# Sink keys of a banded attention: from shared float32r products to float32 products on 16 lanes inside the value step, with new order parameters

## The chip, the cores and the metric

The kernel runs on one core of a Trainium2 chip. The metric is device microseconds (us) of one execution; lower is better. PE is TensorE (PEld its weight loads), DVE is VectorE, ACT is ScalarE, POOL is GpSimd and SP is SyncE, which here issues the DMAs. L12 is line 12 of the kernel before.

## The reference

Two attentions follow each other. The first has 4 batches, 8 heads, 768 positions and head size 64; a query sees the last 128 positions and, besides, the first 4 positions (the sinks):

```python
is_sink = pos[None, :] < int(n_sink)                # n_sink = 4
in_window = (rel >= 0) & (rel < int(window))        # window = 128
scores = np.where(is_sink | in_window, scale * (q @ k.T), -1e9)
attn_out = softmax(scores) @ v                      # per batch and head
```

Its output, heads side by side (512 columns), is the input x of the second: 4 experts, each a causal attention over all 768 positions with its own wq, wk, wv (512x64) and wo (64x512). A gate picks 2 of the 4 experts per position and weights them.

```python
ye = softmax(causal(scale * (x @ wq[e]) @ (x @ wk[e]).T)) @ (x @ wv[e]) @ wo[e]
out += mask[..., None] * w[:, :, kk:kk + 1] * ye
```

## The kernel before

**Units.** The work is cut into 24 units. 16 are of the first kind (`first`, `band_rows`): a batch and a pair of heads. 8 are of the second kind (`second`, `wide_rows`): a batch and a pair of experts; ahead of a batch's first one `values` computes x times wv and the gate, and after its second one `store` multiplies by wo and writes out. Every unit walks over 6 rows of 128 queries.

**A banded row.** TensorE computes the scores of each of two heads (L449): 128 queries against 260 columns, which are 128 positions of the block before, 4 sink keys, and 128 positions of the row's own block. VectorE adds the mask and takes the minimum of the negated scores (L646), ScalarE takes the exponential with its row sum (L651), VectorE inverts the sum (L489, L490), and GpSimd scales the row p by it. For rows 2 to 5 GpSimd first adds the two 128 columns of p to each other (`merge`, L664), since the value products use the block before for both and correct the own block by a difference of values `dv` (L626). Rows 2 and 3, and rows 4 and 5, go on as a pair: `transposed_band` transposes both rows' p on TensorE (L530), copies the result out of PSUM as it is (`evacuate`, L351 on ScalarE or L353 on VectorE) and masked (L533 on VectorE), and multiplies both by values (`acc.add`, L482). A value product has 64 weight columns, and the two heads write the two halves of the partitions of `acc`. It is a float32 product, which stands as two records in the trace.

**The sinks.** The 4 sink columns of rows 2 to 5 are not part of that pair. GpSimd keeps them, scaled, in `psk` (`keep`, L658), which has three copies for a split of float32 into two float32r parts: 3 copies x 4 rows x 2 heads x 4 sinks = 96 columns. Twice per unit (once for row 2, once for rows 3 to 5) TensorE transposes `psk` (L684), ScalarE copies it to `sk` as float32r (L686), VectorE subtracts the rounded part on 32 lanes (L688), and a step of its own, `sinks`, adds one product per row to `acc` (L482, `acc<-sk,vs`): 96 lanes, 128 weight columns, both heads at once, one record each. Its weights `vs` are made by GpSimd once per unit from the first 4 values of every head (`spread`, L617, 96x512), and `psk` is cleared once per unit (L619). `sink_values` makes the copies of those values on 96 lanes once, at the start: two DMAs (L312), two float32 products (L320), copies and differences (L323, L325). When a half unit is complete, `finish` splits `acc` into two float32r parts of x (L334, L339).

**What sets the order.** Each engine runs its instructions in the order in which the program issues them, and `Plan.emit` writes that order out when the program is built: a list scheduler of made-up engine times that always takes the step that could start first, and among those the one of lowest priority number. A step's number is the place of its row in the sequence of units less a lead (`LEAD_S` for scores, `LEAD_E` for exponentials, `LEAD_N` for scaling; `WIDE_S`, `WIDE_E`, `WIDE_N` likewise), or plus `AV_LAG` for the value products; `PREP_*`, `VALUES`, `STORE`, `WP` and `WS` place the preparations, stores and weights. `STAY` is added to the number of a step on TensorE that would change the way in which the array is cut (`mode`), so a larger one lets equal steps gather. `ORD` and `LAST` are the sequences of units of a batch.

Of the kernel before, what the change touches and what calls it, by code (L numbers as in the profile page):

```python
# [29 lines left out]
STAY = 7.6  # L30
# [115 lines left out]
def kernel(  # L146
# [35 lines left out]
             "v2": 1, "y0": 1, "y1": 1, "p": 6, "dv": 2, "pt": 6, "psk": 2, "sk": 2, "vs": 2, "o": 2,  # L182
# [3 lines left out]
        {"space": bass.MemoryType.PSUM} if tag in ("s", "t", "acc") else {}))) for tag, n in rings.items() if tag not in ("kz", "st")}  # L186
# [27 lines left out]
    if banded:  # L214
# [15 lines left out]
        gsel = consts.tile([96, 8], F32, name="gsel")  # L230
        nc.gpsimd.memset(gsel, 1.0)
        for c in range(3):
            g = gsel[c * 32:c * 32 + 32]
            nc.gpsimd.affine_select(out=g, in_=g, pattern=[[-4, 8]], compare_op=OP.is_ge, fill=0.0,
                                    base=0, channel_multiplier=1)
            nc.gpsimd.affine_select(out=g, in_=g, pattern=[[4, 8]], compare_op=OP.is_ge, fill=0.0,
                                    base=3, channel_multiplier=-1)
# [64 lines left out]
    def sink_values():  # L302
        vr = buf("v2", [8, B * HP, D])
        vp = consts.tile([96, B * HP * D], F32R, name="vp")
        copies = consts.tile([8, 12, 8], F32, name="copies")
        nc.gpsimd.memset(copies, 1.0)
        nc.gpsimd.affine_select(out=copies, in_=copies, pattern=[[0, 12], [1, 8]], compare_op=OP.is_equal,
                                fill=0.0, base=0, channel_multiplier=-1)

        def load():  # L310
            for e in range(2):
                nc.sync.dma_start(vr.t[e * 4:e * 4 + 4], bass.AP(tensor=v.tensor, offset=v[0, e].offset,  # L312
                                                               ap=[[D, 4], [2 * S * D, B * HP], [1, D]]))
        ld = plan.step(SINK_VALUES, {SP: 950}, load, new=[vr], fifo="v2", moves=200)
        done = []
        for n in range(0, B * HP * D, 512):
            ns = slice(n, min(n + 512, B * HP * D))
            t = buf("t", [128, 4, 128])
# [201 lines left out]
    def transposed_band(prio, accs, i, ps, normed, value, diff):  # L520

        t = new_t()
        whole, part = buf("pt", [128, 2, 2, 128]), buf("pt", [128, 2, 2, 128])

        def tr():
# [18 lines left out]
        for acc in {id(x): x for x in accs}.values():  # L546
            acc.steps.append(s)
# [373 lines left out]
```

## Time and profile before

| | us |
|---|---|
| median of 3 runs | 473.53 (472.79 to 474.91) |
| the profiled execution: own time | 478.79 |
| its span, first to last instruction | 477.1 |
| PE busy | 451.3 (95%) |
| PEld / DVE / ACT / POOL busy | 388.2 / 344.0 / 320.0 / 276.3 |
| mean granted TensorE clock | 0.982 |

The profiled execution took 1.7 us more than its span, and 5.3 us more than the median. Its span is what all views divide up. Busy times of PE are modelled ends of pipelined products, so the distance from one start to the next tells more of the price of a product than its duration.

### The profile page before, as it was taken

To read this page: it belongs to the slowest core of one execution; us is meant where nothing else is said; L and a number is where in the kernel's file an instruction comes from. 1 tells how busy PE (TensorE), PEld (TensorE's weight loads), DVE (VectorE), ACT (ScalarE), POOL (GpSimd) and SP (SyncE) were. 2 spreads that over 40 slices of the span, in tenths; PEclk is the share of its full clock that TensorE was granted. 3 is DMA by queue.
4 is the path that set the end of the run, shared out by engine and by line. 5 is a ranking of instruction groups with operands and counts; after the bars stand their busy time and mean duration, and the time that the engine had idled before them with its cause. 6 is when DMAs were issued, how large, how long until landed. Compare 5 with 4: busy or idle time off the path is not lost.

```text
span 477.1 us, 11401 instructions
## 1 busy us (share of the span) xinstructions
PE 451.3 (95%) x3732; PEld 388.2 (81%) x3732; DVE 344.0 (72%) x1334; ACT 320.0 (67%) x917; POOL 276.3 (58%) x485
## 2 busy tenths in 40 slices
PE   6998989999899999999989999899999999999996
PEld 4676668898688978998878978799888788998775
DVE  6587786577779787467778878775977975367773
ACT  4778986547759778546758789775577865246640
POOL 8668998345836666526565746762647472015660
PEclk9978999999999999999989999999999999999999
DMA  8858596411635678222424986543112412214012
GB/s 175 160 123 165 134 246 145 101 34 34 145 91 134 170 186 219 61 69 66 101 68 103 211 210 164 119 103 93 40 43 59 103 47 89 63 38 101 0 42 93
DMA packets 95715, 51.89 MB, mean 109 GB/s; under 512 B 84648, under 2 KB 84648, under 8 KB 95656
## 3 DMA queue, kind: packets, MB, share of 16 engines
q1 hardware_dynamic: 95656, 51.16, 45.3%
q8 instruction: 30, 0.49, 0.4%
q14 instruction: 29, 0.24, 0.2%
HBM read 21.01 MB, written 6.29 MB: 57 GB/s over the span
## 4 chain that ended last, share of the span: by engine, by line
PE 69%; DVE 15%; ACT 8%; issue 3%; POOL 2%; DMA 1%; SPq 0%; POOLq 0%; DVEq 0%; ACTq 0%
PE acc L482 16%; PE s L449 14%; PE t L764 12%; PE t L507 10%; PE t L835 6%; PE t L790 6%; DVE p L646 3%; PE t L738 3%; DVE pt L533 2%; PE t L530 2%; ACT pt L351 2%; DVE p L583 2%; ACT p L593 1%; ACT qs L412 1%; ACT p L651 1%
## 5 line engine op out<-in xcount | busy, mean ns | idle before, releaser
L449 PE MATMUL s<-ks,qs 64*128 64x260 f32 (+6 forms) x416 | 109.8, 352 | 3.1 <-DVE st L646 2.2
L651 ACT ACTIVATE p<-p,st 128x260 f32<-128x260 f32 (+1 forms) x192 | 93.9, 497 | 18.5 <-DVE st L646 16.6
L600 POOL TENSOR_TENSOR p<-p,st 128x128 f32<-128x128 f32 (+5 forms) x96 | 87.6, 933 | 3.6 <-POOL st L493 0.2
L593 ACT ACTIVATE p<-p,st 128x128 f32<-128x128 f32 (+5 forms) x96 | 64.0, 668 | 33.0 <-DVE st L583 27.2
L646 DVE CUSTOM_DVE_ANT_0 p<-s,bmask 128x260 f32<-128x260 f32 (+1 forms) x192 | 73.6, 399 | 14.3 <-PE s L449 10.1
L351 ACT ACTIVATE pt<-t 128x512 f32<-128x512 f32 (+1 forms) x104 | 54.9, 536 | 42.3 <-PE t L507 28.4
L449 PEld LDWEIGHTS s<-ks,qs 128*128 128x128 f32 (+1 forms) x416 | 65.0, 203 | 19.9 <-DVE st L583 5.5
L449 PE MATMUL s<-kz,qs 128*128 128x260 f32 (+4 forms) x272 | 79.4, 305 | 0.1
L671 POOL TENSOR_TENSOR p<-p,st 128x256 f32<-128x256 f32 x96 | 65.7, 688 | 17.6 <-DVE st L490 10.0
L507 PE MATMUL t<-ident,p 128*128 128x128 f32 x432 | 65.6, 286 | 3.5 <-DVE ql L416 2.8
L664 POOL TENSOR_TENSOR p<-p 128x256 f32<-128x256 f32 x64 | 46.8, 734 | 34.7 <-ACT p L651 34.5
L493 POOL TENSOR_TENSOR st<-st,gate 128x2 f32<-128x2 f32 x48 | 9.4, 195 | 85.6 <-DVE st L490 77.1
L507 PEld LDWEIGHTS t<-ident,p 128*128 128x128 f32 x432 | 50.9, 146 | 9.9 <-POOL p L600 4.2
L583 DVE CUSTOM_DVE_ANT_0 p<-s,cmask 128x512 f32<-128x512 f32 (+3 forms) x96 | 51.6, 552 | 4.3 <-PE s L449 4.1
L449 PEld LDWEIGHTS s<-kz,qs 128*128 128x128 f32 x272 | 51.9, 191 | 1.7 <-DMA kz<-kl 0.2
L412 ACT ACTIVATE ks<-t 128x768 fp32r<-128x768 f32 (+2 forms) x76 | 38.7, 552 | 17.1 <-PE t L764 13.6
L412 ACT ACTIVATE qs<-t 128x768 fp32r<-128x768 f32 (+1 forms) x48 | 36.4, 758 | 18.6 <-PE t L764 14.9
L482 PE MATMUL acc<-pt,vn 128*64 128x128 f32 x448 | 41.2, 291 | 4.2 <-ACT pt L351 3.4
L482 PE MATMUL acc<-pt,v 128*64 128x128 f32 x672 | 44.5, 280 | 0.3 <-DVE pt L353 0.2
L353 DVE COPY pt<-t 128x512 f32<-128x512 f32 (+1 forms) x56 | 35.4, 632 | 12.8 <-PE t L507 12.5
L482 PEld LDWEIGHTS acc<-pt,v 128*64 128x64 f32 x672 | 36.3, 137 | 7.6 <-issue 3.4
L790 PE MATMUL t<-wvh,x 128*128 128x260 f32 x192 | 38.5, 287 | 0.4 <-DVE st L489 0.4
(106 smaller groups left out, 959.7 us busy)
## 6 DMA issues: line engine op xcount, KB each, us to landing
qs<-ql SPq DMA_DIRECT2D x40, 192.0 KB, 3.8
vn<-in_v_dram SPq DMA_DIRECT2D x32, 192.0 KB, 3.6
out_dram<-o SPq DMA_DIRECT2D x24, 256.0 KB, 2.3
qn<-in_q_dram SPq DMA_DIRECT2D x30, 192.0 KB, 3.3
kn<-in_k_dram SPq DMA_DIRECT2D x30, 192.0 KB, 4.0
ks<-ks SPq DMA_DIRECT2D x24, 197.0 KB, 4.3
kz<-kl SPq DMA_DIRECT2D x24, 197.0 KB, 4.6
ks<-ks SPq DMA_DIRECT2D x16, 192.0 KB, 3.2
```

The costliest lines, as they stand in the source:

```text
L351: nc.scalar.activation(dst(), src(), AF.Copy)
L412: nc.scalar.activation(dst(), src(), AF.Copy, scale=mul)
L449: nc.tensor.matmul(o, lhs, rhs, start=n == 0, stop=n == (2 if self.flat else 1))
L482: nc.tensor.matmul(o if e is None else o[e * 64:e * 64 + 64], lhs, rhs, start=first and e is not None, stop=last and i % 3 == 2)
L507: nc.tensor.transpose(t.t[:, 2 * e + c, :], block(e, c), ident)
L583: nc.vector.tensor_tensor_reduce(out=p.t[:, cs], in0=s.t[:, :(c1 - c0) * 128], in1=mask[:, cs], scale=1.0, scalar=st.t[:, 3, es] if c0 els ...
L593: nc.scalar.activation(x, x, AF.Exp, bias=st.t[:, 0, es], scale=-1.0, accum_out=st.t[:, 1, es])
L600: nc.gpsimd.tensor_mul(x, x, st.t[:, 2, e:e + 1].to_broadcast([128, n * 128]))
L646: nc.vector.tensor_tensor_reduce(out=p.t[:, e, a:], in0=s.t[:, a:RW], in1=row_mask[i][:, a:], scale=1.0, scalar=BIG, op0=OP.add, op1=OP.mi ...
L651: nc.scalar.activation(x, x, AF.Exp, bias=st.t[:, 0, e:e + 1], scale=-1.0, accum_out=st.t[:, 1, e:e + 1])
L671: nc.gpsimd.tensor_mul(x, x, st.t[:, 2, :][:, :, None].to_broadcast([128, 2, z - a]))
L790: nc.tensor.matmul(ps()[:, :VW], X[b, c].t[:, a, qs], W["wv"][w][:, c, :], start=c == 0 and n == 0, stop=c == NCH - 1 and n == 2)
```

## The change

The sinks stay in float32. `psk` becomes a ring of 4 constant tiles of 128x128 that are cleared once at the start; a tile holds, in its first 16 columns, two rows x two heads x 4 sinks, and the other columns stay zero. It is transposed once per pair of rows and copied by `evacuate` on either engine, with no second part. `vs` becomes a ring of 2 constant 128x(4x64) tiles whose first 16 lanes GpSimd fills per unit (16x256 elements). The step `sinks` is gone: `av` of `transposed_band` adds, for each row and head, a float32 product with 64 weight columns, 128 lanes and 128 moving columns, and so waits for the copy `moved_sk` and for `vs` as well. `sink_values` loads 16 lanes with four DMAs and computes nothing. All order parameters change, and one sequence of units: the last batch runs `p0 p1` ahead of its own units 2 and 3 rather than between them. The diff, cut:

```diff
-STAY = 7.6
+STAY = 9.08
...
     rings = {"qn": 2, "kn": 2, "vn": 3, "ql": 1, "kl": 1, "qs": 2, "ks": 2, "kz": 2, "x": 6,
-             "v2": 1, "y0": 1, "y1": 1, "p": 6, "dv": 2, "pt": 6, "psk": 2, "sk": 2, "vs": 2, "o": 2,
+             "v2": 1, "y0": 1, "y1": 1, "p": 6, "dv": 2, "pt": 6, "psk": 4, "sk": 2, "vs": 2, "o": 2,
              "gate": 2, "gates": 1, "st": 6, "s": 3, "t": 3, "acc": 2}
...
-        gsel = consts.tile([96, 8], F32, name="gsel")
...
+        gsel = consts.tile([16, 4], F32, name="gsel")
...
+        sink_ring = {}
+        for tag, shape in (("psk", [128, 128]), ("vs", [128, 4, D])):
+            tiles = [consts.tile(shape, F32, name=f"{tag}{n}") for n in range(rings[tag])]
+            for t in tiles:
+                nc.gpsimd.memset(t, 0.0)
+            sink_ring[tag] = itertools.cycle(tiles)
...
-        vr = buf("v2", [8, B * HP, D])
-        vp = consts.tile([96, B * HP * D], F32R, name="vp")
-        copies = consts.tile([8, 12, 8], F32, name="copies")
...
+        vp = consts.tile([16, B * HP, D], F32, name="vp")
...
-            for e in range(2):
...
-            mm = plan.step(SINK_VALUES, {PE: 870}, lambda ps=ps, ns=ns: nc.tensor.matmul(
...
-            h = plan.step(SINK_VALUES, {ACT: 500}, lambda ps=ps, ns=ns: nc.scalar.activation(vp[:, ns], ps(), AF.Copy),
...
-            done.append(plan.step(SINK_VALUES, {DVE: 600}, lambda ps=ps, ns=ns: nc.vector.tensor_sub(
...
+            for r in range(2):
+                for e in range(2):
+                    nc.sync.dma_start(vp[r * 8 + e * 4:r * 8 + e * 4 + 4],
+                                      bass.AP(tensor=v.tensor, offset=v[0, e].offset, ap=[[D, 4], [2 * S * D, B * HP], [1, D]]))
+        return vp, [plan.step(SINK_VALUES, {SP: 1900}, load, moves=400)]
...
+    def transposed_band(prio, accs, i, ps, normed, value, diff, sinks):
...
+        psk, kept, vs, made_vs = sinks
+        ts, sk = new_t(), buf("sk", [128, 128])
...
+        tt = plan.step(prio, {PE: 109}, lambda: nc.tensor.transpose(ts.t[:, 0, :], psk.t, ident), kept, [ts, sk], [psk])
+        moved_sk = evacuate(prio, lambda: sk.t, lambda: ts.t[:, 0, :], 128, [tt], [ts, sk])
...
-                for c in range(2):
+                for c in range(3):
                     for e in range(2):
-                        acc.add(i + r, e, diff[0](i + r, e) if c else value[0](i + r - 1, e), (part if c else whole).t[:, r, e, :])
+                        if c == 2:
+                            acc.add(i + r, e, vs.t[:, 2 * r + e, :], sk.t, True)
+                        else:
+                            acc.add(i + r, e, diff[0](i + r, e) if c else value[0](i + r - 1, e), (part if c else whole).t[:, r, e, :])
...
+        s = plan.step(prio + AV_LAG, {PE: 1308}, av, [moved, tri, moved_sk, made_vs] + value[1] + diff[1], new,
+                      [whole, part, sk, vs] + value[2] + diff[2] + [acc.b for acc in both if acc.b not in new],
                       fifo="av", mode="cols")
...
-        psk = buf("psk", [128, 3, 4, 2, 4])
-        vs = buf("vs", [96, 8, D], F32R)
+        vs = Buf("vs", lambda: next(sink_ring["vs"]))
...
-            vp = SINKS[0].bitcast(F32)[:, number, :]
-            nc.gpsimd.tensor_mul(vs.t, vp[:, None, :].to_broadcast([96, 8, D]), gsel[:, :, None].to_broadcast([96, 8, D]))
-        made_vs = plan.step(prio0, {POOL: pool_cost(512)}, spread, SINKS[1], [vs], fifo="vs")
-        cleared = plan.step(prio0, {POOL: 150}, lambda: nc.gpsimd.memset(psk.t, 0.0), (), [psk], fifo="psk")
-        kept = []
...
+            nc.gpsimd.tensor_mul(vs.t[:16], vp[:, None, :].to_broadcast([16, 4, D]), gsel[:, :, None].to_broadcast([16, 4, D]))
+        made_vs = plan.step(prio0, {POOL: pool_cost(256)}, spread, SINKS[1], [vs], fifo="vs")
...
-                def keep(i=i, p=p, st=st):
-                    nc.gpsimd.tensor_mul(psk.t[:, :, i - 2], p.t[:, None, :, 128:SW].to_broadcast([128, 3, 2, 4]),
-                                         st.t[:, 2, :][:, None, :, None].to_broadcast([128, 3, 2, 4]))
-                kept.append(plan.step(prio - LEAD_N, {POOL: 190}, keep, [r, cleared], (), [p, st, psk]))
...
+                if i % 2 == 0:
+                    psk = Buf("psk", lambda: next(sink_ring["psk"]))
+
+                def keep(i=i, p=p, st=st, psk=psk):
+                    nc.gpsimd.tensor_mul(psk.t[:, i % 2 * 8:i % 2 * 8 + 8].rearrange("p (e s) -> p e s", e=2), p.t[:, :, 128:SW],
+                                         st.t[:, 2, :][:, :, None].to_broadcast([128, 2, 4]))
+                kept = [plan.step(prio - LEAD_N, {POOL: 190}, keep, [r], [] if i % 2 else [psk], [p, st] + ([psk] if i % 2 else []),
+                                  fifo=None if i % 2 else "psk")]
...
-            for g in ([0] if i == (3 if joined < NB else 2) else [1] if i == NB - 1 else []):
-                ts, sk = new_t(), buf("sk", [96, 128], F32R)
-                tt = plan.step(prio, {PE: 109}, lambda ts=ts: nc.tensor.transpose(
-                    ts.t[:96, 0, :], psk.t.rearrange("p c i e s -> p (c i e s)"), ident), kept[:1] if not g else kept[:], [ts, sk], [psk])
-                h = plan.step(prio, {ACT: 158}, lambda sk=sk, ts=ts: nc.scalar.activation(sk.t, ts.t[:96, 0, :], AF.Copy),
-                              [tt], (), [sk, ts])
-                lw = plan.step(prio, {DVE: 320}, lambda sk=sk, ts=ts: nc.vector.tensor_sub(
-                    sk.t[64:96], ts.t[64:96, 0, :], sk.t[64:96].bitcast(F32)), [h], (), [sk, ts])
...
-                def sinks(span=span, sk=sk, acc=accs[g]):
-                    for ii in span:
-                        lhs = vs.t[:, 2 * (ii - 2):2 * (ii - 2) + 2, :].rearrange("p e d -> p (e d)")
-                        acc.add(ii, None, lhs, sk.t, True)
-                accs[g].steps.append(plan.step(prio, {PE: 50 + 112 * len(span)}, sinks, [lw, made_vs, accs[g].steps[-1]], (),
-                                           [sk, vs, accs[g].b], fifo="av"))
...
-    LEAD_S, LEAD_E, LEAD_N = 6, 1.6, 2.7
-    WIDE_S, WIDE_E, WIDE_N = 7.9, 2.1, 3.3
-    UNIT_1, UNIT_2, AV_LAG, JOIN = 10, 24, 3.8, 0
-    SINK_VALUES = 6
+    LEAD_S, LEAD_E, LEAD_N = 9.36, 3.77, 3.75
+    WIDE_S, WIDE_E, WIDE_N = 8.23, 2.76, 1.78
+    UNIT_1, UNIT_2, AV_LAG = 10.36, 24.87, 3.27
+    SINK_VALUES = 3.68
...
-    LAST = "0 1 2 p0 p1 3 c0 c1"
+    LAST = "0 1 p0 p1 2 3 c0 c1"
...
-    PREP_0, PREP_1, PREP_2, VALUES, STORE = 9.6, 23.9, 24.6, 11.2, 3.8
-    WP, WS = 3.4, 5.8
+    PREP_0, PREP_1, PREP_2, VALUES, STORE = 7.63, 26.46, 22.81, 10.54, 5.79
+    WP, WS = 2.88, 7.16
```

The program's orders show where this moves work. First the start of unit 0's pair of rows 2 and 3 on PE; `psk` is transposed, `v`,`copies` is the product of `sink_values`, `acc<-sk,vs` the sinks. Before:

```order
L320 MATMUL t<-v_262,copies 96x512
L449 MATMUL s<-ks,qs 128x260 x6
L320 MATMUL t<-v_262,copies 96x512
L684 MATMUL t<-ident,psk 96x128
L449 MATMUL s<-ks,qs 128x260 x6
L530 MATMUL t<-ident,p 128x128 x4
L482 MATMUL acc<-pt,vn 64x128 x2
L482 MATMUL acc<-pt,dv 64x128 x2
L482 MATMUL acc<-pt,vn 64x128 x2
L482 MATMUL acc<-pt,dv 64x128 x2
L449 MATMUL s<-ks,qs 128x260 x6
L482 MATMUL acc<-sk,vs 128x128
```

In the changed program, the same place:

```order
L525 MATMUL t<-ident,psk_174 128x128
L519 MATMUL t<-ident,p 128x128 x4
L437 MATMUL s<-ks,qs 128x260 x6
L470 MATMUL acc<-pt,vn 64x128 x2
L470 MATMUL acc<-pt,dv 64x128 x2
L470 MATMUL acc<-sk,vs_182 64x128 x2
L470 MATMUL acc<-pt,vn 64x128 x2
L470 MATMUL acc<-pt,dv 64x128 x2
L470 MATMUL acc<-sk,vs_182 64x128 x2
L437 MATMUL s<-ks,qs 128x260 x6
L525 MATMUL t<-ident,psk_175 128x128
```

The two products of `sink_values` are gone, and the sink products stand inside the run of value products instead of behind the next row's scores.

Next, on PE, rows of unit p1 of batch 2 (`v_4722` before, `v_4891` changed: its values) among preparations (`qn`, `kn`) and rows of other units. Before:

```order
L482 MATMUL acc<-pt,v_4722 64x128 x14
L738 MATMUL t<-ident,kn 128x128 x3
L507 MATMUL t<-ident,p 128x128 x4
L449 MATMUL s<-ks,qs 128x512
L449 MATMUL s<-kz_204,qs 128x512
L449 MATMUL s<-ks,qs 128x128
L449 MATMUL s<-kz_204,qs 128x128
L449 MATMUL s<-ks,qs 128x512
L449 MATMUL s<-kz_204,qs 128x512
L482 MATMUL acc<-pt,v_4722 64x128 x4
```

In the changed program, the same place:

```order
L720 MATMUL t<-ident,kn 128x128 x3
L495 MATMUL t<-ident,p 128x128 x18
L437 MATMUL s<-ks,qs 128x260
L437 MATMUL s<-kz_206,qs 128x260
L470 MATMUL acc<-pt,v_4891 64x128 x18
L437 MATMUL s<-ks,qs 128x260
L437 MATMUL s<-kz_206,qs 128x260
L437 MATMUL s<-ks,qs 128x260
L437 MATMUL s<-kz_206,qs 128x260
```

Transposes and value products of several steps now stand together: runs of 18 where runs of 4 and 14 stood. Over all of PE's order there were 76 runs of value products, sinks apart, and there are now 63.

Last, POOL's first instructions (`gsel` is the selector for `vs`, `cmask` the causal mask, `copies` the weights of the products of `sink_values`). Before:

```order
L234 AFFINE_SELECT gsel<-gsel 32x8
L236 AFFINE_SELECT gsel<-gsel 32x8
L252 MEMSET cmask 128x768
L253 AFFINE_SELECT cmask<-cmask 128x128
L261 MEMSET tril 128x16
L262 AFFINE_SELECT tril<-tril 128x16
L306 MEMSET copies 8x96
L307 AFFINE_SELECT copies<-copies 8x96
L619 MEMSET psk 128x96 x2
```

In the changed program, the same place:

```order
L233 AFFINE_SELECT gsel<-gsel 16x4
L235 AFFINE_SELECT gsel<-gsel 16x4
L241 MEMSET psk_174 128x128
L241 MEMSET psk_175 128x128
L241 MEMSET psk_176 128x128
L241 MEMSET psk_177 128x128
L241 MEMSET vs_182 128x256
L241 MEMSET vs_183 128x256
L257 MEMSET cmask 128x768
L258 AFFINE_SELECT cmask<-cmask 128x128
L266 MEMSET tril 128x16
L267 AFFINE_SELECT tril<-tril 128x16
L618 TENSOR_TENSOR dv<-vn 128x4x64 x2
```

The clearing of `psk` and `vs` has moved to the start, and the second and third group of `gsel` and `copies` are gone.

## Rows read from the trace of the kernel before

**Rows 1.** The page, busy time, share of the span and instructions of each engine

```profile
PE 451.3 (95%) x3732; PEld 388.2 (81%) x3732; DVE 344.0 (72%) x1334; ACT 320.0 (67%) x917; POOL 276.3 (58%) x485
```

**Rows 2.** Windows: stretch, us, busy by engine (PE PEld DVE ACT POOL), PEclk, DMA

```profile
0.00:40.00 40.00, 34.56 (x222) 24.61 (x222) 27.47 (x116) 27.71 (x90) 30.21 (x75) 0.91 0.77 153
40.00:80.00 40.00, 34.58 (x314) 27.52 (x315) 32.34 (x135) 34.73 (x114) 35.70 (x65) 0.96 0.85 189
...
440.00:477.00 37.00, 32.74 (x277) 25.47 (x275) 22.88 (x71) 15.65 (x39) 16.90 (x23) 1.00 0.12 44
```

**Rows 3.** Windows, shorter stretches, the same columns

```profile
20.00:30.00 10.00, 10.00 (x62) 6.12 (x59) 6.94 (x26) 6.54 (x22) 6.68 (x11) 0.70 0.60 131
...
50.00:60.00 10.00, 8.81 (x80) 6.28 (x76) 9.09 (x39) 9.70 (x33) 10.00 (x17) 1.00 0.66 153
60.00:70.00 10.00, 8.11 (x84) 6.60 (x85) 8.21 (x35) 8.55 (x28) 9.91 (x20) 1.00 1.10 247
```

**Rows 4.** Timeline of PE: start us, us, what, records; a pair's value products, three sinks

```profile
61.03 0.39 PE L482 MATMUL acc<-pt,vn 128*64 128x128 f32 x4
61.25 0.39 PE L482 MATMUL acc<-pt,dv 128*64 128x128 f32 x4
61.56 0.56 PE L482 MATMUL acc<-sk,vs 96*128 96x128 f32 x3
61.95 0.62 PE L507 MATMUL t<-ident,p 128*128 128x128 f32 x4
```

**Rows 5.** Timeline of PE, from scores into value products, and one sink product

```profile
68.36 0.28 PE L449 MATMUL s<-ks,qs 128*128 128x260 f32 x1
68.48 0.28 PE L449 MATMUL s<-kz,qs 128*128 128x260 f32 x1
68.69 0.44 PE L482 MATMUL acc<-pt,vn 128*64 128x128 f32 x4
...
69.71 0.33 PE L482 MATMUL acc<-sk,vs 96*128 96x128 f32 x1
69.88 0.34 PE L449 MATMUL s<-ks,qs 128*128 128x260 f32 x1
```

**Rows 6.** Timeline of PE at the start, the products of `sink_values`

```profile
21.60 1.09 PE L320 MATMUL t<-v,copies 8*96 8x512 f32 x2
22.62 0.64 PE L449 MATMUL s<-ks,qs 64*128 64x260 f32 x6
23.19 1.35 PE L320 MATMUL t<-v,copies 8*96 8x512 f32 x2
24.47 0.45 PE L684 MATMUL t<-ident,psk 128*96 128x128 f32 x1
```

**Rows 7.** Timeline of PE, from value products into transposes

```profile
376.01 0.66 PE L482 MATMUL acc<-pt,v 128*64 128x128 f32 x8
376.60 0.71 PE L507 MATMUL t<-ident,p 128*128 128x128 f32 x4
```

**Rows 8.** Groups by form: what, count | busy us, mean ns | idle before

```profile
L671 POOL TENSOR_TENSOR p<-p,st 128x256 f32<-128x256 f32 x80 | 49.0, 615 | 11.2 <-DVE st L490 7.4 <-ACT p L651 2.2 <-ACT vp L323 1.3
...
L617 POOL TENSOR_TENSOR vs<-vp,gsel 96x512 fp32r<-96x512 f32 x16 | 16.6, 1041 | 0.0
...
L658 POOL TENSOR_TENSOR psk<-p,st 128x24 f32<-128x24 f32 x64 | 14.4, 228 | 5.0 <-DVE st L490 3.7 <-ACT x L334 0.9
...
L688 DVE TENSOR_TENSOR sk<-t,sk 32x128 fp32r<-32x128 f32 x32 | 9.3, 289 | 1.0
...
L686 ACT ACTIVATE sk<-t 96x128 fp32r<-96x128 f32 x32 | 8.5, 267 | 1.3 <-PE t L684 1.3
...
L619 POOL MEMSET psk<- 128x96 f32 x16 | 2.8, 176 | 11.8 <-PE t L684 11.8
```

**Rows 9.** Waits: who waited for whom, us in total, times, longest

```profile
PEld acc L482 <- ACT pt L351: 5.9, 10, 1.2
```

**Rows 10.** Timeline of SP, DMA issues of the sink values

```profile
9.13 0.80 SPq L312 DMA_DIRECT2D v<-in_v_dram  x2
```

More of the change, by code (lines that the diff above doesn't have):

```diff
@@ L185 @@
     pools = {tag: ctx.enter_context(tc.tile_pool(name=tag + "_", bufs=n, **(
-        {"space": bass.MemoryType.PSUM} if tag in ("s", "t", "acc") else {}))) for tag, n in rings.items() if tag not in ("kz", "st")}
+        {"space": bass.MemoryType.PSUM} if tag in ("s", "t", "acc") else {}))) for tag, n in rings.items() if tag not in ("kz", "st", "psk", "vs")}
     consts = ctx.enter_context(tc.tile_pool(name="consts", bufs=1))
@@ L229 @@
                                 base=0, channel_multiplier=-1)
-        gsel = consts.tile([96, 8], F32, name="gsel")
+        gsel = consts.tile([16, 4], F32, name="gsel")
         nc.gpsimd.memset(gsel, 1.0)
[L232 to L237, printed above, removed]
+        nc.gpsimd.affine_select(out=gsel, in_=gsel, pattern=[[-4, 4]], compare_op=OP.is_ge, fill=0.0,
+                                base=0, channel_multiplier=1)
+        nc.gpsimd.affine_select(out=gsel, in_=gsel, pattern=[[4, 4]], compare_op=OP.is_ge, fill=0.0,
+                                base=3, channel_multiplier=-1)
+        sink_ring = {}
[4 more added lines that the diff above has]
+            sink_ring[tag] = itertools.cycle(tiles)
     else:
@@ L626, in differences @@
                 nc.gpsimd.tensor_sub(dv.t[:, :, e, :], value[2][0].t[:, 2:, e, :], value[2][0].t[:, 1:NB - 1, e, :])
-        differ = joined < NB and plan.step(prio0 - LEAD_E, {POOL: 1390}, differences, value[1], [dv], value[2], fifo="dv")
+        differ = plan.step(prio0 - LEAD_E, {POOL: 1390}, differences, value[1], [dv], value[2], fifo="dv")
         accs, rows = [Acc(), Acc()], {}
@@ L700 @@
+            else:
+                rows[i] = (p, nm, kept)
+                if i % 2:
+                    before = rows[i - 1]
+                    transposed_band(prio, [accs[(i - 1) // 3], acc], i - 1, [before[0], p], [before[1], nm], value,
+                                    (lambda i, e: dv.t[:, i - 2, e, :], [differ], [dv]), (psk, before[2] + kept, vs, made_vs))
+                    finish(prio, accs[i // 4], i // 4)
     X, X_READY, Y, Y_READY, V2, V2_READY, WT, WT_READY = ({} for _ in range(8))
@@ L745, in first @@
         if banded:
-            band_rows(prio0, step, pair, value, b * HP + hp, finish, 2 if b >= JOIN else NB)
+            band_rows(prio0, step, pair, value, b * HP + hp, finish)
         else:
```

44 lines of the change are left out of this document (10 added, 34 removed).

## The prediction

> **What bounds the kernel now.** I read the busy shares first, then the windows, then the timeline of TensorE for prices, then the groups of the engines that feed it. TensorE is busy 451.3 of 477.1 us [rows 1], far ahead of VectorE, ScalarE and GpSimd. So the time is TensorE's work plus 25.8 us in which it stands. The windows tell where it stands [rows 2]: 5.4 us in the first 40 (which holds the start), 5.4 us between 40 and 80, 4.3 us in the last 37, and by difference 10.7 us spread over the 360 us between. From 50 to 70 us GpSimd is busy 10.00 and 9.91 of 10 us, ScalarE up to 9.70 [rows 3]: there the banded rows of batches 0 and 1 run with no expert work to fill TensorE, and GpSimd is the pace. Elsewhere TensorE is the pace, and an edit on it counts in full.
>
> The sum is made against the profiled execution, 478.8 us (span 477.1). That is 5.3 us above the median of 473.5, so I carry the difference, not the total, over to the median.
>
> **TensorE: what is added.** Each of the 32 pair steps (16 units, 2 pairs) gets 4 more value products, 128 in all. Four records of such products, which are two products, start 0.22 us after the four before them [rows 4]; so a product costs 0.109 us, and 128 cost 14.0 us. Their form, 128 lanes, 64 weight columns and 128 moving columns, is that of the row; that 112 lanes hold zeros changes nothing in the form.
>
> **A rule against it.** The rows show 0.109 us for a float32 product on half the columns, and 0.13 us for a float32r sink product that serves both heads [rows 4]. The Trainium skill (FP8 and Floating Point Precision, Matmul Precision, TensorE Precision Notes) says that true FP32 takes 4 passes through the array. At 2.4 GHz four passes of 128 columns would be 0.213 us, so by that page 128 products taken one by one would cost an estimated 27 us. The trace has half of that per product, because the two heads' halves run side by side; the measurement decides, and the sum goes by 14.0 us.
>
> **TensorE: what is removed.** A `sinks` step of three products holds TensorE for 0.39 us from its first start to the next work's [rows 4], one of one product for 0.17 us [rows 5]. That is 0.56 us in each of 16 units, 9.0 us. Not all of it comes back. Entering the sinks costs 0.09 us (61.47, the end of the spacing, to 61.56), which goes. But where value products are followed by transposes, these start 0.15 us late (376.01 plus 8 records of 0.0545 is 376.45, next start 376.60), and four of them then take 0.71 us against 0.62 after sinks [rows 4, 7]. Per step 0.15 net would be lost, 4.8 us in all. So between 4.2 and 9.0 us are saved; I take the middle, 6.6, since scores, which follow sinks as often, show neither end.
>
> The four records of `sink_values` go too: 1.02 us and 1.28 us to the next start, 2.3 us [rows 6]. They stand in TensorE's row without a gap, so I count them; if the pace there is another engine's, they are worth 0.
>
> **TensorE: what is moved.** The new order has 63 runs of value products where 76 stood. A run costs 0.09 us to enter (0.21 us from the last scores to the first product, against 0.12 between scores) [rows 5] and 0.15 us to leave [rows 7]: 13 times 0.24 is 3.1 us saved, or 4.3 with the slower transposes behind. The sum for TensorE is 14.0 - 6.6 - 2.3 - 3.1 = **+2.0 us**, between -1.6 and +6.7.
>
> **GpSimd.** `spread` shrinks from 96x512 at 1041 ns to 16x256. No row shows 16 lanes; the nearest is 128x256 at 615 ns, the bounds are 0 and 1041, and I take 615: 16 times 0.43 is 6.8 us. The clears of `psk` in the units, 16 times 176 ns, are 2.8 us. `keep` writes 8 columns for 24, 64 times at 228 ns; a multiply that small is mostly fixed, so I take 30 ns off, 2.1 us (bounds 0 and 14.4) [rows 8]. Together 11.7 us, of which 6 of 16 units' part, 4.4 us, falls ahead of 80 us. The six clears at the start, at 176 ns per 128x96, are by their columns (1024 for 96) an estimated 1.9 us; some `gsel` and `copies` work goes there in exchange, so I count 0, bounded by 1.9.
>
> **VectorE and ScalarE.** VectorE loses 32 differences, 9.3 us, ScalarE 32 copies, 8.5 us [rows 8], and 32 new copies of 128x128, at about 0.27 us each, are shared between the two: 9.2 us less in all. Both lie beside TensorE's work, so alone they are worth nothing; if that cover went they would be worth their share. The copies of `vs`'s source go as well, small.
>
> **DMA.** SP issues four DMAs for the sink values where two took 0.80 us [rows 10], and the loads of wv now stand ahead of them on SP. Behind them wait the values of unit 1. If the sink values land late, `spread` holds GpSimd's queue, and the first pair step waits for it: between 0 and about 1 us, once. I take 0, since the products and copies that stood between landing and `spread` are gone.
>
> **Where stalls go.** GpSimd's 4.4 us fall where it is the pace for part of the time; of the 5.4 us between 40 and 80 I take back 2.5 (bounds 0 and 4.4). The next to be late there is ScalarE. The new leads issue scores earlier. Counting TensorE's products between a row's scores and its first transposes, at the spacings of the trace, the median distance grows from about 8.2 to 9.0 us, an estimate; more work lies ahead of each wait. Of the other 16.1 us outside the tail (5.4 + 10.7) I take back a quarter, 4.0. The bounds are +3 (new stalls) and -8. The tail of 4.3 us keeps its order and stays.
>
> **Sum.** +2.0 - 2.5 - 4.0 = -4.5 us: the profiled execution would go from 478.8 to 474.3, and the median from 473.5 to **469.0 us**.
>
> **The rivals.** *TensorE paces all, no change:* the stalls are set by chains through exponentials and scaling that neither the 11.7 us on GpSimd nor the leads shorten. Then only the +2.0 stays, 475.5, or about 473 if the price of runs is at its better bound. For it: 95% busy. Against: GpSimd full for 20 us. Time 471.2 to 475.9.
>
> *A larger gain:* from 20 to 30 us TensorE is busy without a gap, yet its granted clock is 0.70 [rows 3], so some 6 of the 10 us run at 1.2 GHz for 2.4, worth 3 us. This is where the products of `sink_values` stand, on 8 lanes. If the clock stays up without them, and half rather than a quarter of the stalls goes (-8), the sum is 2.0 - 2.5 - 8 - 3 = -11.5: 462. Against it: idle time ahead may lower the clock as well.
>
> *Slower: the pair step waits for its sink copy.* `av` now waits also for `moved_sk` and `vs`, and behind it on TensorE stands everything, the value steps of all rows first. The copy takes 0.27 us [rows 8] and, queued ahead of the pair's own copy on ScalarE or VectorE, makes that one as late. It decides where less than about 0.3 us of other work stands between transposes and value products. Value products already waited for ScalarE's copies 10 times, 5.9 us [rows 9]. If all 32 steps lose 0.27 us, that is 8.6 us more than the no-change case's +2.0: 484; if half do, 480. Against it: in the order `psk` is transposed before the pair's p, and scores stand before the products.
>
> *Slower: the halves take turns.* Were the two heads' halves not side by side, each product would cost 0.218 us, 14 us more: 483. That is the page's four passes in full; rows 4 speak against it.
>
> **How the numbers follow.** A measurement of this kernel can tell about 0.5%, 2.4 us, from no change. Forecast (465.5 to 471.1) 0.46; larger gain (459 to 465.5) 0.18; no change 0.22; sink copy 0.12; taking turns 0.02. Faster is 0.64, same 0.22, slower 0.14. The range runs from 461.5, leaving out the better part of the bounds, to 476.0, leaving out the slower cases.
>
> **What would show it.** Right: value products at 0.109 us and `spread` near 0.6 us; GpSimd about 12 us less busy; TensorE's busy time within 3 us of 451; fewer stalls between 40 and 80. A TensorE stall before `acc` that ends with `sk` shows the slower rival; a granted clock near 1.00 from 20 to 30 us shows the larger gain. The forecast is wrong if TensorE's idle time does not fall, or if its work grows by more than 5 us.

## The result and the profile after

The changed kernel takes 457.59 us in the median of 4 runs (456.61 to 459.52), the kernel before, run beside it, 474.22. The ratio is 0.9645, with a 95% interval of 0.9584 to 0.9706. The forecast was 469.0 us and its range began at 461.5: the sign was right, the gain of 16.6 us was more than three times the 4.5 that had been forecast, and the time lies outside the range. Two executions that are marked as slow, 479.9 us of the kernel before and 1058 us of the run with the old `STAY` below, are left out of the ranges and counts given here.

The busy line of the changed kernel's page answers to [rows 1]:

```profile
PE 440.7 (97%) x3920; PEld 390.3 (86%) x3920; DVE 330.3 (72%) x1309; ACT 316.7 (69%) x906; POOL 265.3 (58%) x469
```

TensorE has 188 records more and is busy 10.6 us less. Of a span of 456.0 us it stands for 15.3 us, where it stood for 25.8. The windows answer to [rows 2] and [rows 3], with the same columns:

```profile
0.00:40.00 40.00, 33.58 (x279) 24.76 (x281) 30.18 (x133) 31.19 (x104) 35.30 (x84) 1.00 0.92 172
40.00:80.00 40.00, 38.18 (x345) 33.30 (x346) 27.23 (x118) 31.16 (x96) 31.98 (x58) 0.96 0.83 180
419.00:456.00 37.00, 32.70 (x277) 25.66 (x276) 22.88 (x70) 15.81 (x40) 17.39 (x23) 1.00 0.12 44
20.00:30.00 10.00, 9.51 (x109) 7.47 (x109) 8.06 (x39) 9.69 (x35) 10.00 (x17) 1.00 0.97 194
50.00:60.00 10.00, 9.85 (x98) 8.41 (x99) 6.37 (x29) 8.91 (x33) 8.24 (x16) 0.83 1.06 241
```

Idle time from 40 to 80 us falls from 5.4 to 1.8 us, in the last 37 us it stays (4.3 for 4.3), and at the start it is 6.4 for 5.4. Between 80 us and the last 37, in which the kernel before lost 10.7 us, 2.8 are left. From 20 to 30 us the granted clock is 1.00 where it was 0.70.

The timeline of TensorE (start us, us, operation, records) shows a pair step with its new sink products; it answers to [rows 4]:

```profile
62.03 0.28 PE L437 MATMUL s<-kz,qs 128*128 128x260 f32 x1
62.24 0.44 PE L470 MATMUL acc<-pt,vn 128*64 128x128 f32 x4
62.51 0.39 PE L470 MATMUL acc<-pt,dv 128*64 128x128 f32 x4
62.73 0.39 PE L470 MATMUL acc<-sk,vs 128*64 128x128 f32 x4
62.94 0.39 PE L470 MATMUL acc<-pt,vn 128*64 128x128 f32 x4
```

The sink products take 0.21 us per four records, as the value products beside them do: the price of 0.109 us per product was right. The groups by form (count | busy us, mean ns) answer to [rows 8]:

```profile
L654 POOL TENSOR_TENSOR psk<-p,st 128x8 f32<-128x8 f32 x64 | 12.9, 202 | 2.8 <-DVE st L478 1.7 <-PE t L495 0.9
L611 POOL TENSOR_TENSOR vs<-vp,gsel 16x256 f32<-16x256 f32 x16 | 9.7, 604 | 0.0
L339 ACT ACTIVATE sk<-t 128x128 f32<-128x128 f32 x21 | 5.8, 275 | 1.4 <-PE t L525 1.4
L341 DVE COPY sk<-t 128x128 f32<-128x128 f32 x11 | 3.2, 289 | 2.3 <-PE t L525 2.2
```

**Where the 20.8 us between the two profiled executions went.** From TensorE's first product to its last there were 468.6 us before and 447.8 after. I split the distances between starts into three: idle stretches of 0.1 us and more (gaps), half of the time at the lower of the clock's two levels (1.2 for 2.4 GHz), and the rest, which I call work; it holds the changes from one kind of work to another and waits under 0.1 us. The sums are good to about 0.2 us. The time ahead of the clock's first rise, at 20.5 us before and 15.9 after, counts as lower too: the views show 1.00 there, but transposes start 0.24 us apart in it, against 0.11 later. The expectations below add the 4.1 and 3.9 us ahead of the first product to the gaps: their 21.3 and 11.0 are the 17.2 and 7.0 here.

| us | before | after | difference | forecast |
|---|---|---|---|---|
| work | 435.3 | 433.4 | -1.9 | +2.0 |
| gaps | 17.2 | 7.0 | -10.2 | -6.5 |
| lower clock | 16.2 | 7.4 | -8.8 | 0 |

### The profile page after: what moved, and what is told of

It is laid out like the page before. It is cut to its first block, busy times and chain, and to the rows that moved or that the text cites. A ratio compares the mean times of both kernels' runs of the same rounds, so it can differ in the third digit from the quotient of the medians.

```text
span 456.0 us, 11781 instructions
## 1 busy us (share of the span) xinstructions
PE 440.7 (97%) x3920; PEld 390.3 (86%) x3920; DVE 330.3 (72%) x1309; ACT 316.7 (69%) x906; POOL 265.3 (58%) x469
## 4 chain that ended last, share of the span: by engine, by line
PE 81%; ACT 10%; DVE 3%; POOL 2%; issue 2%; DMA 0%; ACTq 0%; POOLq 0%; DVEq 0%
PE acc L470 19%; PE s L437 17%; PE t L746 15%; PE t L495 10%; PE t L772 7%; PE t L817 7%; PE t L720 3%; ACT p L643 2%; ACT pt L339 2%; PE t L519 2%; ACT p L588 2%; ACT ks L400 2%; ACT qs L400 2%; DVE pt L522 1%; PE t L525 1%
## 5 line engine op out<-in xcount | busy, mean ns | idle before, releaser
L588 ACT ACTIVATE p<-p,st 128x256 f32<-128x256 f32 (+5 forms) x96 | 64.1, 670 | 28.5 <-DVE st L578 23.8
L638 DVE CUSTOM_DVE_ANT_0 p<-s,bmask 128x260 f32<-128x260 f32 (+1 forms) x192 | 72.2, 399 | 10.9 <-PE s L437 9.4
L437 PEld LDWEIGHTS s<-ks,qs 128*128 128x128 f32 (+1 forms) x416 | 64.5, 198 | 17.3 <-issue 7.1
L339 ACT ACTIVATE pt<-t 128x512 f32<-128x512 f32 (+1 forms) x109 | 57.6, 530 | 30.6 <-PE t L495 21.9
L437 PE MATMUL s<-kz,qs 128*128 128x260 f32 (+4 forms) x272 | 78.3, 304 | 0.0
L495 PE MATMUL t<-ident,p 128*128 128x128 f32 x432 | 63.1, 278 | 2.9 <-ACT qs L400 1.3
L495 PEld LDWEIGHTS t<-ident,p 128*128 128x128 f32 x432 | 48.9, 141 | 9.6 <-issue 2.8
L618 POOL TENSOR_TENSOR dv<-vn 128x256 f32<-128x256 f32 x32 | 22.8, 731 | 29.9 <-PE acc L470 29.9
L341 DVE COPY pt<-t 128x512 f32<-128x512 f32 (+1 forms) x51 | 33.0, 647 | 9.7 <-PE t L495 9.1
```

Of the source, the lines that this page charges most:

```text
L339: nc.scalar.activation(dst(), src(), AF.Copy)
L437: nc.tensor.matmul(o, lhs, rhs, start=n == 0, stop=n == (2 if self.flat else 1))
L495: nc.tensor.transpose(t.t[:, 2 * e + c, :], block(e, c), ident)
L588: nc.scalar.activation(x, x, AF.Exp, bias=st.t[:, 0, es], scale=-1.0, accum_out=st.t[:, 1, es])
L638: nc.vector.tensor_tensor_reduce(out=p.t[:, e, a:], in0=s.t[:, a:RW], in1=row_mask[i][:, a:], scale=1.0, scalar=BIG, op0=OP.add, op1=OP.mi ...
```

## The experiments

**Two by two: sinks and order apart.** The first kernel is the one before with all order parameters of the change; the second is the changed one with all parameters of before.

```diff
-STAY = 7.6
+STAY = 9.08
...
-    LEAD_S, LEAD_E, LEAD_N = 6, 1.6, 2.7
+    LEAD_S, LEAD_E, LEAD_N = 9.36, 3.77, 3.75
...
```

> The sinks as before (float32r, a step of their own), with all order parameters of the change. If the order carries the gain (theory order), most of the 16.6 us is here: 458 to 463 us, with the idle time of TensorE near the 15.3 us of the change and hardly a stretch at the lower clock. If the new sink code carries it (theory sinks: less work for GpSimd, ScalarE and VectorE, no products of sink_values), this is near the kernel before: 469 to 475 us. If the two only work together, it lies between, 463 to 469.

> The new sinks with the order parameters of before. Theory order: 470 to 476 us, since TensorE gets 14 us of products and loses about 9 to 12. Theory sinks: 458 to 463 us. Together with the run that has the old sinks and the new order it gives a table of two by two.

The old sinks in the new order take 468.73 us (ratio 0.9900, 0.9863 to 0.9938), the new sinks in the old order 480.3 (1.0103, 1.0056 to 1.0149). Alone the order brings 6 us and the sinks cost 5.5; together they bring 16.6. So 16 us lie in neither part: the two act on each other, as the first expectation's third case had it; the second run lies above both of its theories. The kernel before, timed beside each group of runs, had medians from 474.2 to 476.1 us, so medians of different groups compare to about 2 us. The timeline of the new sinks in the old order shows one such place (the bracket is the idle time before, and its releaser):

```profile
197.46 0.27 PE L525 MATMUL t<-ident,psk 128*128 128x128 f32 x1
...
197.57 0.60 PE L519 MATMUL t<-ident,p 128*128 128x128 f32 x4
...
197.77 0.29 DVE L341 COPY sk<-t 128x128 f32<-128x128 f32 x1 [0.79 <-PE t L525]
198.21 0.69 DVE L522 TENSOR_TENSOR pt<-t,own 128x512 f32<-128x512 f32 x1
...
198.93 0.60 ACT L339 ACTIVATE pt<-t 128x512 f32<-128x512 f32 x1 [0.46 <-DVE pt L522]
...
199.58 0.44 PE L470 MATMUL acc<-pt,vn 128*64 128x128 f32 x4 [1.41 <-ACT pt L339]
```

The pair step stands right behind its transposes. The mask product on VectorE and ScalarE's copy read the same `t` one after the other, so the products start 2.0 us after the transposes do, and TensorE stands for 1.41 us. The sink copy holds nothing up here: it has ended, at 198.06, when the transposes end, at 198.17, and the mask product follows at 198.21. In the waits (us in total, times, longest) of the new sinks in the old order it is the largest entry of TensorE and of its weight loads; [rows 9] has 5.9 us for the kernel before:

```profile
PE acc L470 <- ACT pt L339: 7.4, 8, 1.4
PEld acc L470 <- ACT pt L339: 12.1, 17, 1.6
...
PEld acc L470 <- ACT sk L339: 0.3, 2, 0.2
```

The last line is all that waits for a sink copy itself. The trace has eight stalls of 0.1 us and more ahead of banded value products, 6.7 us in all; in one of them, at 49.99 us, a sink copy stands between the transposes and the mask product, which starts 0.2 us late.

The changed kernel has the entry of the weight loads at half of the 5.9 us of the kernel before:

```profile
PEld acc L470 <- ACT pt L339: 2.9, 9, 0.8
```

**What the sink products cost in place.** The loop over `c` in the pair step runs over two parts instead of three.

```diff
-                for c in range(3):
+                for c in range(2):
...
```

The rest of the edit marks the last product of a row as the last; transposes and copies of the sinks stay.

> The change without its 128 sink products, in the same order (the output lacks the sinks' values for rows 2 to 5). If TensorE paces the kernel, their 14.0 us at 0.109 us each come off in full: 443 to 446 us. If TensorE waits for others at these places, less: 450 us or more. It prices the term of the sum that spoke against the change.

448.65 us (ratio 0.9452, 0.9421 to 0.9483): 128 products, 14.0 us by their spacing, cost 9.0 us of the time, between the two cases of the expectation. Without them the gaps grow from 7.0 to 11.2 us: some of the added products stand where TensorE would otherwise wait.

**The products of `sink_values` and the clock.** Two 8-lane products of 512 columns are put back, ahead of the first two transposes of `psk`, which write over their result.

```diff
...
+            if odd:
+                nc.tensor.matmul(ts.t.rearrange("p c n -> p (c n)")[:96], ident[:8, :96],
+                                 SINKS[0][:8].rearrange("p u d -> p (u d)")[:, :512], start=True, stop=True)
             nc.tensor.transpose(ts.t[:, 0, :], psk.t, ident)
...
```

> The change with two float32 products of 8 lanes and 512 columns added at the start, ahead of the first two transposes of the sink tile, as sink_values had them; their results are overwritten. If such products bring the lower clock of the kernel before between 20 and 30 us (theory clock), the granted clock falls there in most runs and the time is 2 to 4 us above the change: 460 to 462. If not, only their own time of about 1 us is seen, or nothing: 457 to 459, and the clock stays up.

458.98 us, and in the profiled execution the clock stays at its full level from 20.4 us, where it first rises, to the last products. The two stand there at 21.0 and 26.0 us; in the kernel before they stood at 21.6 and 23.2, and the clock fell at 23.9. So products of this form do not pull the clock down where they stand 5.0 us apart; 1.6 us apart was not tried.

**GpSimd's relief taken back.**

```diff
...
+            nc.gpsimd.tensor_copy(scratch, cmask[:, :256])
             vp = SINKS[0][:, number, :]
```

> The changed kernel with one more GpSimd copy of 128x256 in each of the 16 banded units, just ahead of the spread of the sink values; the order of TensorE, VectorE and ScalarE is that of the changed kernel. At about 0.6 us each this gives GpSimd back some 10 of the 11.7 us that the change was to take from it, 3 to 4 of them before 80 us. Theory A (the forecast's step: GpSimd is the pace from 40 to 80 us, so its relief is worth about 2.5 us): 459.5 to 461.5 us, with the growth in the window 40 to 80. Theory B (what counts is the distance between transposes and value products on TensorE, GpSimd has slack): 457.0 to 458.5 us, TensorE's idle time within 1.5 us of the 15.3 of the changed kernel.

458.62 us (ratio 0.9641, 0.9570 to 0.9713), with the idle time at 15.7 us. The copies took less than expected:

```profile
L612 POOL COPY scratch<-cmask 128x256 f32<-128x256 f32 x16 | 6.4, 398 | 0.0
```

GpSimd's busy time grew by 5.4 us, so half of the relief was given back, not most of it. That half moved the median by 1.0 us, inside the spread of the runs: this half of GpSimd's relief is not where the gain is, and the other half was not tried.

**One group of parameters at a time.** In order: the new leads, unit spacings and value lag alone in the otherwise old order; the old `STAY` in the otherwise new one; the old order with the value steps due later. The first and the third diff are against the new sinks in the old order, the second against the changed kernel.

```diff
-    LEAD_S, LEAD_E, LEAD_N = 6, 1.6, 2.7
-    WIDE_S, WIDE_E, WIDE_N = 7.9, 2.1, 3.3
-    UNIT_1, UNIT_2, AV_LAG = 10, 24, 3.8
+    LEAD_S, LEAD_E, LEAD_N = 9.36, 3.77, 3.75
+    WIDE_S, WIDE_E, WIDE_N = 8.23, 2.76, 1.78
+    UNIT_1, UNIT_2, AV_LAG = 10.36, 24.87, 3.27
```

> The new sinks with the old order parameters except the leads of scores, exponentials and factors, the spacing of the units and the lag of the value steps, which are the new ones (preparation, weights, stay, last batch's order stay old). Counted on TensorE's order with prices of the trace, the blocks whose value products come within 1.5 us of work after their transposes are 18 of 64 with all old parameters, 8 with all new, 7 here; TensorE changes its kind of work 438, 423 and 435 times. Theory A (the leads give the distance, and the distance is what the new sinks needed): 460 to 467 us, the waits of value products for their copies fall from about 27 us to under 9. Theory B (each group of parameters brings its share, none decides): 472 to 476 us, and the waits stay above 15 us.

```diff
-STAY = 9.08
+STAY = 7.6
```

> The changed kernel with the old price for leaving a kind of work (7.6 for 9.08), all else as changed. The blocks with under 1.5 us of work before their value products stay at 8 of 64, but TensorE changes its kind of work 460 times for 423. Theory A (distance decides and a change of kind costs next to nothing): 457 to 459.5 us. Theory B (a change of kind costs about 0.15 us, as 73.9 us for 495 of them in the trace of before and 63.6 for 422 in that of after): 37 more, 5.5 us, so 462 to 465 us, with TensorE's idle time about the same.

```diff
-    UNIT_1, UNIT_2, AV_LAG = 10, 24, 3.8
+    UNIT_1, UNIT_2, AV_LAG = 10, 24, 10
```

> The new sinks with all old order parameters but one: the value steps are due later (lag 10 for 3.8). The blocks with under 1.5 us of work before their value products fall from 18 of 64 to 8, as in the changed kernel, while TensorE changes its kind of work 474 times for 438. Theory A (what held the new sinks up under the old order is the missing distance): the value products' waits for their copies fall from about 27 us to under 12, and against 480.3 us the time falls by these 15 less 5 for the changes of kind: 468 to 473 us. Theory B (the waits come from what stands ahead of the copies on ScalarE and VectorE, wherever the products stand): waits stay above 18 us, 478 to 485 us.

472.29, 472.97 and 477.28 us: the first lies in the range of theory B, the second beyond both theories, the third between them. In the third the waits of value products and their weight loads for copies sum to 22.6 us, where the new sinks in the old order have 28.2: above 18, as its theory B had it. (The 495 changes of kind in the second expectation are not the 465 of the table below, which counts in the program's order.) One parameter, `STAY`, took back 15.4 of the 16.6 us, where 37 changes of kind at 0.15 us would be 5.5. My count was too narrow: it looked at 64 blocks of banded value products, while the waits in these three traces also stand before the expert attention's blocks. From here on I count all 160 blocks, "close" being those with under 1.5 us of other work, priced by the spacings of the trace, between their transposes and their first value product.

**The kernel before once more, and neighbours of the changed order.**

> The kernel before once more, for a second profile of it: how much of the lower-clock time and of TensorE's idle time in the first profile (478.8 us, 5 above the median) belongs to that one execution. Theory A (the clock's lower stretches are the draw of one execution): time 472 to 476 us, 3 to 6 us less time at 1.2 GHz than in the first profile, TensorE's gaps of 0.1 us and more within 1 us of the first's 21.3. Theory B (they belong to the kernel): a span again near 477, with lower-clock stretches at the same places.

478.85 us. The lower-clock stretches stand at the same places again (first full clock at 20.7 us, then drops at 24.1, 41.2, 129.9 and 242.6 us; in the first profile 20.5, 23.9, 41.0, 129.7, 242.4), and from 20 to 30 us the granted clock is 0.71. So they are no accident of one execution, as theory A had it. But this execution has the same mean granted clock as the first profile, 0.982, and of the 57 executions timed beside the experiments 43 have a higher one: they belong to a case that recurs, not to every execution.

```diff
-STAY = 9.08
+STAY = 9.0
```

> The changed kernel with the price for leaving a kind of work at 9.0 for 9.08, a step of 1 in 100. 1402 lines of TensorE's order differ from the changed kernel's, the kinds change 444 times for 423, the blocks with under 1.5 us of work before their value products stay 8 of 64 (under 2 us: 13 for 10). Theory A (the order's gain comes from what the parameters mean, longer leads and fewer changes; small steps cost little): 457 to 462 us. Theory B (the gain belongs to one order that fits, and any other order loses most of it): 466 to 473 us, with gaps on TensorE of 17 us and more for the 11.0 of the changed kernel.

```diff
-STAY = 9.08
+STAY = 10
```

> The changed kernel with the same price at 10 for 9.08, a step of 1 in 10 the other way. 491 lines of TensorE's order differ, the kinds change 430 times for 423, 6 blocks of 64 for 8 have under 1.5 us of work before their value products. Theory A (what the parameters mean): 456 to 460 us. Theory B (one order fits): 463 to 472 us.

```diff
-    UNIT_1, UNIT_2, AV_LAG = 10.36, 24.87, 3.27
+    UNIT_1, UNIT_2, AV_LAG = 10.96, 24.87, 3.27
...
```

> The changed kernel with the banded units spaced 10.96 for 10.36 apart, the price for leaving a kind 8.59, the score lead 9.44 and the preparation lead 27.25. 1521 lines of TensorE's order differ, but the counts are like the changed kernel's or better: 425 changes of kind for 423, 6 blocks for 8 with under 1.5 us of work before their value products, none for 1 with under 1 us. Theory A (the two counts carry the time): 455 to 461 us. Theory B (one order fits, whatever the counts): 465 to 473 us.

466.51, 459.67 and 457.89 us. A step of 1 in 100 loses 9 us, one of 1 in 10 loses 2, and an order that differs in 1521 lines loses nothing. So neither theory holds as put: the parameters' size says little, but it is not one lucky order either. In these runs the counts over all 160 blocks go with the time.

**A test of the counts, stated ahead.** Two new orders with 433 and 436 changes of kind, and 23 and 61 close blocks; a third with about the changed kernel's counts.

```diff
-    LEAD_S, LEAD_E, LEAD_N = 9.36, 3.77, 3.75
+    LEAD_S, LEAD_E, LEAD_N = 9.6, 3.77, 3.75
```

> The changed kernel with the scores' lead at 9.6 for 9.36. All 160 blocks of value products counted now, those with under 1.5 us of work after their transposes are 31 for the changed kernel's 35, the changes of kind 426 for 423. Theory A (changes of kind and close blocks together; fitted to the eight kernels with the new sinks that have run, 0.22 us per change and 0.60 us per us by which blocks fall short of 1.6 us): 457.0 us, 455 to 460. Theory B (the changed kernel's order is a single fit, any other loses): 462 us or more. If it comes in under 456.5 us it is better than both kernels.

```diff
-    UNIT_1, UNIT_2, AV_LAG = 10.36, 24.87, 3.27
+    UNIT_1, UNIT_2, AV_LAG = 9.66, 25.38, 3.48
...
```

> The changed kernel with other spacing and leads of the units (9.66 and 25.38; 27.92 and 24.15 for their preparation; wide exponentials 2.86; value lag 3.48): 433 changes of kind for 423, but only 23 blocks of 160 for 35 have under 1.5 us of work after their transposes. Theory A (both counts): 458.3 us, 455 to 462. Theory B (the changes of kind alone, 0.35 us each as fitted): 465.2 us.

```diff
-    WIDE_S, WIDE_E, WIDE_N = 8.23, 2.76, 1.78
+    WIDE_S, WIDE_E, WIDE_N = 7.75, 2.76, 1.78
...
```

> The changed kernel with smaller leads (scores 9.31, factors 3.55, wide scores 7.75, value lag 3.34, stay 9.17): 436 changes of kind, about as many as the kernel with more kinds and far blocks has, but 61 blocks of 160 have under 1.5 us of work after their transposes. Theory A (both counts): 472.9 us, 469 to 477, with the gaps ahead of value products above 4 us where the changed kernel has 1.7. Theory B (the changes of kind alone): 466.3 us, and the gaps ahead of value products stay near 2 us.

459.39, 461.44 and 474.13 us, each within the bounds of the theory of both counts (457.0, 458.3, 472.9), if up to 3.1 us off its middle; by the changes of kind alone the last two would have been 465.2 and 466.3, with 1 us between them. There are 12.7. Of these 7.3 are work and 7.6 gaps in the profiled executions; ahead of value products the gaps are 3.3 and 6.9 us, ahead of transposes 4.2 and 8.1. TensorE's waits ahead of value products, first with 23 close blocks, then with 61:

```profile
PE acc L470 <- ACT pt L339: 1.7, 3, 0.9
...
PE acc L470 <- DVE pt L341: 0.8, 1, 0.8
```

```profile
PE acc L470 <- ACT pt L339: 2.9, 4, 0.9
PE acc L470 <- DVE pt L341: 2.1, 4, 1.0
...
PE acc L470 <- DVE pt L522: 1.1, 4, 0.3
```

All orders side by side (work and gaps as in the table above, from each profiled execution):

| kernel | changes of kind | close of 160 | work | gaps | median us |
|---|---|---|---|---|---|
| before | 465 | 29 | 435.3 | 17.2 | 474.2 |
| old sinks, new order | 441 | 29 | 435.6 | 13.8 | 468.7 |
| new sinks, old order | 438 | 66 | 443.3 | 18.1 | 480.3 |
| **changed** | 423 | 35 | 433.4 | 7.0 | 457.6 |
| wider units | 425 | 33 | 433.8 | 7.8 | 457.9 |
| scores earlier | 426 | 31 | 433.4 | 8.4 | 459.4 |
| `STAY` 10 | 430 | 30 | 434.3 | 8.7 | 459.7 |
| more kinds, far | 433 | 23 | 433.6 | 9.7 | 461.4 |
| `STAY` 9.0 | 444 | 53 | 437.4 | 12.8 | 466.5 |
| new leads only | 435 | 54 | 439.5 | 16.2 | 472.3 |
| `STAY` 7.6 | 460 | 58 | 439.4 | 16.1 | 473.0 |
| near values | 436 | 61 | 440.9 | 17.3 | 474.1 |
| value steps later | 474 | 40 | 442.3 | 17.7 | 477.3 |

With the new sinks, the five orders with at most 433 changes and at most 35 close blocks take 457.6 to 461.4 us; the six others take 466.5 to 480.3, with 4 to 10 us more work and 6 to 11 us more gaps. None that was tried beats the changed kernel; the order with wider units can't be told from it.

## Why the prediction was wrong

The median fell by 16.6 us where 4.5 had been forecast. By the table above, work is 3.9 of the missing 12.1 us and gaps 3.7; the remaining 4.5 are the clock's share of the median's gain, an estimate by difference.

**Right: the bound, the sign, the prices.** TensorE is the pace. A sink product cost 0.109 us, `spread` 604 ns for 615, `keep` 202 for 198, GpSimd's busy time fell by 11.0 us for 11.7 (64 times 30 ns is 1.9, where the sum has 2.1). VectorE and ScalarE lost 13.7 and 3.3 us, more than the 9.2 together; what that is worth was not tried. The tail kept its idle time. One sign that I had named failed: TensorE's busy time was to stay within 3 us of 451 and fell to 440.7. The rival in which the halves take turns falls: four records start 0.21 us after the four before, and the records of the two heads start 0.007 us apart. The Trainium skill (FP8 and Floating Point Precision, Matmul Precision, TensorE Precision Notes) has four passes for true FP32; as before, the trace has half of that per product, since two products share the 0.21 us.

**Wrong: the sum of separate terms.** This is the main step that failed. I priced the sinks as if the order stood (+5.1 for products, sinks and `sink_values`) and the order as if the sinks stood (-3.1 for 13 fewer runs). Measured apart, the sinks under the old order add 8.0 us of work and the new order under the old sinks 0.3: both worse than forecast. Together they take 1.9 away. The old parameters put the new pair steps close behind their transposes (66 close blocks for 29); the new ones undo that (35), and drop the changes of kind to 423, which the old sinks did not reach in the one new order they were run in (441).

**Wrong: the stalls.** I took back 2.5 us between 40 and 80 for GpSimd's relief and a quarter of the rest. There 3.6 came back, while the new sinks in the old order, which have GpSimd's whole relief, still stand 4.8 of the 5.4 us there; and of the 10.7 us between 80 us and the last 37, 7.9 came back. My ground was the distance from scores to transposes. The gaps stand ahead of several kinds of work: ahead of transposes they fell from 8.7 to 3.6 us, ahead of value products from 5.1 to 1.7, ahead of scores from 3.1 to 1.6. Only 2.4 us of those ahead of transposes had ended with GpSimd's p; most of the others end with an instruction of VectorE or ScalarE that reads one of the three `t` buffers (`ql`, `qs`, `pt`), a wait that the forecast did not have. TensorE's waits before, then after:

```profile
...
PE acc L482 <- ACT pt L351: 3.4, 4, 1.0
PE t L507 <- DVE ql L416: 2.8, 2, 1.4
PE s L449 <- DVE st L646: 2.2, 5, 0.9
PE t L530 <- POOL p L664: 1.6, 1, 1.6
```

```profile
...
PE t L495 <- ACT qs L400: 1.3, 3, 0.4
PE acc L470 <- ACT pt L339: 0.8, 2, 0.6
PE t L495 <- POOL p L668: 0.8, 1, 0.8
```

The close blocks tell the orders of the new sinks apart (ahead of value products the gaps are 10.2 us in the old order and 1.7 in the new); from the kernel before to the changed one they do not fall (29 and 35).

**Wrong: the clock at nothing.** 8.8 us of the profiled difference are time at the lower level. Of this some 4.5 us is the profiled execution of before being that much slower than the median of its runs: its 57 executions beside the experiments range from 472.5 to 479.4 us; the 14 with a mean granted clock of 0.982, like the profiled one, took 478.0 to 479.4, the seven with 0.996 took 472.7 to 473.4. At 0.996 the changed kernel took 457.7 and 459.5: some 15 of the 16.6 us are there at equal clocks. The clock at 1.00 from 20 to 30 us, which I had named as the sign of the larger gain, came; the cause I had given it, the products of `sink_values`, is not borne out by the two products put back, though these stood further apart. What holds the clock up there stays open: no run changed it alone. The mean granted clock leaves out the time ahead of the first rise, 2.3 us of the difference in the table; in the run with the extra copies, whose order on TensorE is the changed kernel's, that rise came at 20.9 us rather than 15.9, so this part can be a draw.

**The slower rival** did not come, and the 480.3 us of the new sinks in the old order, where I had given 480, are no sign of it; the agreement is luck: waits for a sink copy are 0.3 us there, one of eight stalls has a sink copy ahead of the pair's own, and against the kernel before the gaps grow by 0.9 us and the work by 8.0. (In the rival of no change, "about 473" should be 474.3: with runs at 4.3 the sum is +0.8.)

**What stays open.** The two counts were fitted to the new sinks. The kernel before and the old sinks in the new order lie some 7 us above that fit, so the sinks themselves bring something at equal counts; which of their parts was not tried. Nor do the counts settle each order: a straight line through the eleven orders with the new sinks misses single ones by up to 5 us. The new parameters were run with the old sinks as they are, to two decimals, and a step of 1 in 100 cost the changed kernel 9 us: how much of the 16 us is that these numbers fit the new steps, and what an order found for the old sinks would bring, was not tried. The count of close blocks goes with the gaps and with work alike, and was not varied alone within one otherwise fixed order.

## What to carry to other kernels

When a change alters both the steps and the parameters of an order, price them together: build the new order and count on it how often the busiest engine changes its kind of work, and how many steps follow too closely on the one that feeds them. Count the short distances, for all steps of that form, beside their median. A busy-time saving on an engine that looks full in a window can be worth little: ask first with whose work the pace-setting engine's waits end.

## What the runs showed of the hardware

The lower-clock stretches of the kernel before came at the same places, within 0.3 us, in two profiled executions with a mean granted clock of 0.982; in timed executions of the same kernel it went from 0.982 (478.0 to 479.4 us) to 0.996 (472.7 to 473.4). When TensorE first reached its full clock varied, from 15.4 to 25.0 us over the kernels. On GpSimd a 128x256 copy took 0.40 us and a multiply of that form 0.61; on 16 lanes the multiply took as long (604 ns for 613). And 128 products of 0.109 us cost 9.0 us of time, not 14.0, on an engine that is busy 97%: here a third of added work stood in waits that would otherwise show.
